# Three edits to the expert stage of a fused attention, feed-forward and expert kernel

## The chip, the cores and the metric

The kernel runs on one core of a Trainium2 chip. The metric is the time of one launch on the device in microseconds. Five engines work side by side, each through its own instructions in order: TensorE (PE, matrix products and transposes), VectorE (DVE), ScalarE (ACT), GpSimd (POOL, here mainly the issuer of indirect DMAs) and SyncE (SP, the issuer of the plain DMAs). 16 DMA engines move data between the chip's memory and the core.

## The reference, cut to what matters

The change touches the third of three parts. Attention with pooled queries gives 1152 tokens of 512 numbers; a gated feed-forward layer follows; its result `x` goes through eight experts, of which each token uses two:

```python
def _moe2_ref(x, w_gate, w_noise, noise, w1, w2):      # x 1152 x 512, 8 experts, hidden 1024
    noisy_logits = x @ w_gate + np.log1p(np.exp(x @ w_noise)) * noise
    top2 = np.argpartition(-noisy_logits, 2, axis=1)[:, :2]
    top2_w = ...                                       # softmax over the two
    for e in range(E):
        for k in range(2):
            mask = top2[:, k] == e
            h = np.maximum(x[mask] @ w1[e], 0.0)
            out[mask] += top2_w[mask, k, None] * (h @ w2[e])
```

## The kernel before

Routing puts the tokens of each expert into blocks of 128, and the expert stage works through a fixed list of units, `SEQ` (L953). A unit is one expert's weights with one set of blocks. Kind P has two blocks, S one, Q one block and a half block (64 tokens), H a half block alone. The list names for each unit its kind and its place among the columns of the index tables, which routing fills at run time; so the work of a unit depends on its kind only. The first two P work on the experts with most tokens; P 0 to 3, Q 0 to 2, S 0 and H 0 to 3 follow in the order of the list. Before the change that order is P, P, P0, H0, Q0, H1, P1, H2, Q1, H3, P2, Q2, P3, S0. Further units, behind a branch (L1296), run only when routing needs them.

**Weights.** An expert has 4 MB, loaded as eight pieces of 512 KB (`e_dma`, L983): pieces 0 to 3 are the first layer (256 hidden columns each), 4 to 7 the second. The buffers of raw weights are two sets of eight; unit u uses set u % 2, so unit u + 2 can be loaded into a piece's buffer once unit u has read it. Full blocks don't use the raw weights: `wsplit` (L1039) splits a piece into a rounded high part (`w_hi`, a cast on ACT, L106) and a low part (`w_lo`, a subtraction on DVE, L1037), into a ring of six pairs of buffers, and each product is three passes, high by high, high by low, low by high (`PASS`). Half blocks use the raw weights in plain float32, with 64 columns of the array for each of two halves.

**Order.** `units` (L1212) writes out the order of all engines' work by hand: whatever is called earlier stands earlier in each engine's queue. Pieces of P, Q and S form one list, `todo`; while piece n is computed, piece n + LEAD (five on) is split, and for P and S (not Q) the load of the same piece of unit u + 2 is issued right after (L1217 to L1220). H units are not in that list.

**A P or S or Q unit** runs eight pieces: first layer in 0 to 3 (`up_pair` for P, `up_one` for Q and S), second in 4 to 7 (`down`). Q and S transpose the hidden values (`h_trans`, two calls of four transposes; ACT casts the high part, DVE subtracts the low). After piece 5, `next_x` transposes the tokens of the next unit, computes its weights and gathers the tokens of unit u + 3. After piece 4, `finish` scales the previous unit's result on DVE into a buffer, one for even units and one for odd, and POOL adds it to the output by an indirect DMA; each such scatter waits for the one before.

**A half** (in H or Q) has the steps `up_half` (L1142; 16 matmuls twice, each followed by a relu on ACT), `hh_trans` twice (L1153; two transposes each, then a copy) and `down_half` (L1166; 32 matmuls). `up_half` reads raw pieces 0 to 3, `down_half` raw pieces 4 to 7; after each, `reload` issues the loads of these four pieces for unit u + 2. An H does `up_half` twice, `reload`, `hh_trans`, `next_x`, `hh_trans`, `finish`, `down_half`, `reload`. A Q does `up_half` after piece 3, `hh_trans` after piece 5, `down_half` after piece 7.

**Banks.** PSUM has eight banks of 512 float32 per partition: two shared for transposes (`bank`, taken in turn), two for the first layer (`pbank("ph")`, in turn), four for the second (`pbank("py")`). The half's relu results lie in `hs0` and `hs1`, one buffer each, which Q's first layer uses too.

Of the kernel before, what the change touches and what calls it, by code (L numbers as in the profile page):

```python
# [21 lines left out]
def fused_kernel(ctx, tc, q, k, v, w_gate, w_val, w_out, rms_g,  # L22
                 r_gate, r_noise, noise, e_w1, e_w2, out, dbg=None):
    nc = tc.nc
    P = 128
    B, H, S, D = q.shape
# [10 lines left out]
    pe, dve, act, pool, sp = nc.tensor, nc.vector, nc.scalar, nc.gpsimd, nc.sync  # L37
# [896 lines left out]
    def r_index(pl):  # L934
# [11 lines left out]
        for z, kind in enumerate((KH, KQ2)):  # L946
# [3 lines left out]

    RAW = []
    REG = {}
    SEQ = [("P", None)] * 2 + [("P", 0), ("H", 0), ("Q", 0), ("H", 1), ("P", 1), ("H", 2), ("Q", 1), ("H", 3), ("P", 2),  # L953
                               ("Q", 2), ("P", 3), ("S", 0)]
    SEQ = [(a, {"P": ((KP, r), (KP2, r)), "Q": ((KQ, r), (KQ2, r)), "S": ((KS, r),), "H": ((KH, r),)}[a]) for a, r in SEQ]
    NU1 = len(SEQ)
    SEQ += [("P", ((KP, r), (KP2, r))) for r in range(NSTAT[KP], NA)]
    SEQ += [("P", ((KQ, r), (KQ2, r))) for r in range(NSTAT[KQ], NE)]
    SEQ += [("S", ((KS, r),)) for r in range(NSTAT[KS], NE)] + [("S", ((KH, r),)) for r in range(NSTAT[KH], NE)]

    def kind(u):
        return SEQ[u][0]

    def nblk(u):
        return len(SEQ[u][1])

    def half(u, k):
        return kind(u) == "H" or kind(u) == "Q" and k == 1
# [48 lines left out]
    def experts():  # L1017
# [21 lines left out]
        def wsplit(u, i):  # L1039
            w_hi(u, i)  # L1040
            w_lo(u, i)
# [21 lines left out]
        def bank():  # L1063
            tb[0] += 1
            if tb[0] % 2:
                return pst.tile([P, 512], F32, name="xt", tag="T")
            return ptab.tile([P, 512], F32, name="xt", tag="tab")

        def pbank(nm):
            if pm:  # L1070
                return pm[0].tile([P, 512], F32, name=nm, tag=nm, bufs=4 if nm == "py" else 2)
            return ps.tile([P, 512], F32, name=nm, tag="gv0" if nm == "py" else "po", bufs=2)
# [32 lines left out]
        def up_pair(u, i, j):  # L1105
            if j == 0:
                PL[u, i] = pbank("ph")
            w = [x.rearrange("p a (b f) -> p (a b) f", f=256) for x in W[u, i]]
            o = PL[u, i][:, 256 * j:256 * j + 256]
            for z, (a, c) in enumerate(PASS):  # L1110
                for d in range(4):
                    pe.matmul(o, w[a][:, d, j * P:j * P + P], XT[u][c][:, d], start=z + d == 0, stop=z == 2 and d == 3)  # L1112

        def up_evac(u, i):
            hi, lo = (x[:, 2 * i:2 * i + 2].rearrange("p a c -> p (a c)") for x in t_hTT(u))
            act.activation(hi, PL[u, i], AF.Relu)
            dve.scalar_tensor_tensor(lo, PL[u, i], 0.0, hi.bitcast(F32), op0=ALU.max, op1=ALU.subtract)
# [14 lines left out]
        def down(u, i, k):  # L1132
            if (u, "y", k) not in PL:
                PL[u, "y", k] = pbank("py")
            w, x = W[u, i], HTT[u]
            f0 = 2 * (i - 4)
            for z, (a, c) in enumerate(PASS):
                for d in range(2):
                    pe.matmul(PL[u, "y", k], x[c][:, f0 + d, k * P:k * P + P], w[a][:, d],  # L1139
                              start=i == 4 and z + d == 0, stop=i == 7 and z == 2 and d == 1)  # L1140

        def up_half(u, a):  # L1142
            k = nblk(u) - 1
            t = pbank("ph")
            for d in range(4):
                for g in range(2):
                    pe.matmul(t[HB * g:HB * g + HB, 0:256], XH[u][:, d],
                              RAW[u % 2][2 * a + g].rearrange("p a (b f) -> p (a b) f", f=256)[:, d],
                              start=d == 0, stop=d == 3)
            HS[u, "h", a] = mo.tile([P, 512], F32, name="hs", tag=f"hs{a}", bufs=1)[:, 0:256]  # L1150
            act.activation(HS[u, "h", a], t[:, 0:256], AF.Relu)

        def hh_trans(u, a, eng):  # L1153
            if a == 0:
                HH[u] = X2[:, 4 + u % 2, 0:8 * HB].rearrange("p (c t) -> p c t", t=HB)
            pt = bank()
            for j in range(2):
                pe.transpose(pt[:, j * P:j * P + P], HS[u, "h", a][:, j * P:j * P + P], ident)
            o = HH[u][:, 4 * a:4 * a + 4].rearrange("p (g j) t -> p j g t", g=2)
            i = pt[:, 0:2 * P].rearrange("p (j g t) -> p j g t", j=2, g=2)  # L1160
            if eng is act:
                act.copy(o, i)
            else:
                eng.tensor_copy(o, i)

        def down_half(u):  # L1166
            k = nblk(u) - 1
            y = PL[u, "y", k] = pbank("py")
            for c in range(8):
                for g in range(2):  # L1170
                    pe.matmul(y[HB * g:HB * g + HB, 0:256], HH[u][:, c], RAW[u % 2][4 + c // 2][:, c % 2, 256 * g:256 * g + 256],
                              start=c == 0, stop=c == 7)

        def piece(u, i):
            if i >= 4:
                for k in range(nblk(u)):
                    if not half(u, k):
                        down(u, i, k)
            elif kind(u) == "P":
                up_pair(u, i, 0)  # L1180
                up_pair(u, i, 1)
                up_evac(u, i)
            else:
                up_one(u, i)
# [27 lines left out]
        def units(u0, u1, skip=0):  # L1212
            todo = [(u, i) for u in range(u0, u1) if kind(u) != "H" for i in range(8)]

            def split(n):
                if n < len(todo):
                    v, j = todo[n]  # L1217
                    wsplit(v, j)
                    if v + 2 < u1 and kind(v) != "Q":
                        wload(v + 2, j)  # L1220

            def reload(u, js):
                if u + 2 < u1:
                    for j in js:
                        wload(u + 2, j)

            def next_x(u):
                if u + 1 < u1:
                    x_trans(u + 1)
                    weight(u + 1)  # L1230
                    if u + 3 < u1:
                        gather_x(u + 3)

            if not skip:
                for u in range(u0, min(u0 + 2, u1)):
                    gather_x(u)
                    for i in range(8):
                        wload(u, i)
                for n in range(LEAD):
                    split(n)  # L1240
                x_trans(u0)
                weight(u0)
                if u0 + 2 < u1:
                    gather_x(u0 + 2)
            n_ = 0
            for u in range(u0, u1):
                last = u == u1 - 1
                if kind(u) == "H":
                    up_half(u, 0)
                    up_half(u, 1)  # L1250
                    reload(u, range(4))
                    hh_trans(u, 0, dve)
                    next_x(u)
                    hh_trans(u, 1, dve)
                    finish(u - 1)
                    down_half(u)
                    reload(u, range(4, 8))
                    continue
                for i in range(8):
                    if n_ < skip:  # L1260
                        n_ += 1
                        continue
                    piece(u, i)
                    if kind(u) != "P":
                        if i == 2:
                            h_trans(u, 0)
                        if i == 4 - last:
                            h_trans(u, 1)
                    if kind(u) == "Q":
                        if i == 3:  # L1270
                            up_half(u, 0)
                            up_half(u, 1)
                            reload(u, range(4))
                        if i == 5:
                            hh_trans(u, 0, act)
                            hh_trans(u, 1, act)
                        if i == 7:
                            down_half(u)
                            reload(u, range(4, 8))
                    if i == 5:  # L1280
                        next_x(u)
                    if u > max(u0, 1) and i == (1 if last else 5 if kind(u) == "S" else 4):
                        finish(u - 1)
                    split(n_ + LEAD)
                    n_ += 1
            finish(u1 - 1)
# [278 lines left out]
```

## Time and profile before

| | us |
|---|---|
| median of three runs (812.81 to 816.31) | 815.96 |
| the profiled execution | 819.15 |
| its span | 817.4 |
| PE busy | 767.9 (94%) |
| DVE busy | 525.4 (64%) |
| ACT busy | 378.0 (46%) |
| POOL busy | 257.0 (31%) |

The profile is of one execution; the span runs from its first to its last instruction, and the profiled execution's own time adds what lies around it. Busy shares are averages over stages with different limits. "PEclk" is the granted clock of TensorE as a share of 2.4 GHz; it is 1 (2.4 GHz) or 0.5 (1.2 GHz) at any moment, so a share between is a mean over a stretch. A line such as L1158 is a line of the kernel before; arrows read "written from read".

### The profile page before, as it was taken

The page shows a single profiled execution, that of the slowest core. Times are in us where ns is not written, and L with a number is a line of the kernel's source. Part 1 is how long each engine was busy: PE and PEld are TensorE (multiplying, and loading weights), DVE is VectorE, ACT ScalarE, POOL GpSimd, SP SyncE. Part 2 cuts the span into 40 slices and gives each one's busy share as a digit, 9 for nine tenths or more (in the row PEclk, how much of TensorE's full clock was granted, in tenths as well). Part 3 has the DMA queues.
Part 4 walks back from the last instruction along what each step waited for, and adds up shares of the span by engine and source line. Part 5 has one row for each costly group of instructions (what it writes and reads, how often), then busy time and mean ns, then how long its engine had stood idle before and what let it go on. Part 6 is the DMA issues. An engine that isn't in the chain of part 4 may idle for free. (4 is left out here: it accounts for less than half of the span.)

```text
span 817.4 us, 13258 instructions
## 1 busy us (share of the span) xinstructions
PE 767.9 (94%) x5008; PEld 630.6 (77%) x5008; DVE 525.4 (64%) x791; ACT 378.0 (46%) x770; POOL 257.0 (31%) x221
## 2 busy tenths in 40 slices
PE   5999999999999899999999999999998899799993
PEld 4877777787776689988888899979976686488792
DVE  6677678688779865765686545697644354345572
ACT  3556566565667535331333243545434244234451
POOL 7457356358514222221223100102232122221121
PEclk9999999999999999999999999999999999889998
DMA  7354232230133213331231016639979969892612
GB/s 213 89 153 138 60 102 73 59 102 15 45 118 103 64 41 103 103 103 52 87 120 55 1 53 208 218 131 342 341 202 292 309 205 313 278 335 59 201 18 39
DMA packets 72728, 113.28 MB, mean 139 GB/s; under 512 B 7281, under 2 KB 37551, under 8 KB 72656
## 3 DMA queue, kind: packets, MB, share of 16 engines
q1 hardware_dynamic: 67504, 101.55, 38.4%
q0 software_dynamic: 5152, 10.80, 6.1%
q8 instruction: 41, 0.67, 0.3%
q14 instruction: 31, 0.25, 0.1%
HBM read 98.16 MB, written 9.85 MB: 132 GB/s over the span
## 5 line engine op out<-in xcount | busy, mean ns | idle before, releaser
L536 PE MATMUL gv<-XN,ws 128*128 128x256 f32 (+2 forms) x912 | 165.1, 331 | 0.9 <-POOL ws L402 0.9
L536 PEld LDWEIGHTS gv<-XN,ws 128*128 128x128 f32 x912 | 143.8, 189 | 15.0 <-issue 1.8
L1037 DVE TENSOR_TENSOR wz<-raw,wz 128x1024 fp32r<-128x1024 f32 x80 | 96.4, 1223 | 66.2 <-ACT wz L106 65.7
L193 DVE TENSOR_REDUCE Ql<-s 128x1 fp32r<-128x1152 f32 x72 | 97.3, 1355 | 57.2 <-PE s L188 35.3
L204 ACT ACTIVATE et<-st 128x288 f32<-128x288 f32 x288 | 103.5, 417 | 41.3 <-PE st L203 38.9
L1139 PE MATMUL py<-wz,hTT 128*128 128x512 f32 x384 | 98.3, 410 | 0.0
L202 PE MATMUL st<-QH,KT 128*128 128x288 f32 x288 | 92.3, 335 | 2.4 <-ACT et L204 1.0
L106 ACT CAST wz<-raw 128x1024 fp32r<-128x1024 f32 x80 | 81.7, 1046 | 26.9 <-DMA raw<-in_moe_w_dram 21.7
L402 POOL TENSOR_TENSOR ws<-wm,ws 128x1024 fp32r<-128x1024 f32 x18 | 43.9, 2438 | 154.4 <-ACT ws L401 139.5
L1139 PEld LDWEIGHTS py<-wz,hTT 128*128 128x128 f32 x384 | 73.4, 196 | 16.4 <-issue 1.2
L557 PE MATMUL po<-ws,hT 128*128 128x512 f32 x324 | 83.2, 395 | 2.2 <-DVE X L562 2.1
L203 PE MATMUL st<-QlT,KT 128*128 128x288 f32 x288 | 81.8, 298 | 0.0
L229 PE MATMUL av<-et,v 128*64 128x288 f32 x576 | 77.4, 412 | 0.5 <-ACT xT L234 0.5
L202 PEld LDWEIGHTS st<-QH,KT 128*128 128x128 f32 x288 | 54.8, 190 | 21.9 <-issue 12.3
L557 PEld LDWEIGHTS po<-ws,hT 128*128 128x128 f32 x324 | 58.9, 188 | 14.2 <-DVE X L562 3.2
L217 DVE TENSOR_TENSOR es<-es,et 128x576 f32<-128x576 f32 x64 | 62.0, 968 | 1.5
L229 PEld LDWEIGHTS av<-et,v 128*64 128x64 f32 x576 | 38.4, 137 | 27.7 <-issue 3.9
L1112 PEld LDWEIGHTS ph<-xgT,wz 128*128 128x128 f32 x480 | 56.0, 188 | 1.3 <-issue 1.2
L1112 PE MATMUL ph<-xgT,wz 128*128 128x256 f32 x480 | 56.6, 279 | 0.0
L203 PEld LDWEIGHTS st<-QlT,KT 128*128 128x128 f32 x288 | 55.2, 192 | 0.1
L1202 POOL DMA_INDIRECT out_dram<-yo,sidx x16 | 26.3, 1645 | 90.1 <-DVE yo L1201 55.1
L546 ACT CAST hT<-sl 128x256 fp32r<-128x256 f32 (+2 forms) x38 | 18.9, 497 | 74.6 <-DVE sl L545 74.6
(280 smaller groups left out, 1143.9 us busy)
## 6 DMA issues: line engine op xcount, KB each, us to landing
raw<-in_moe_w_dram SPq DMA_DIRECT2D x112, 512.0 KB, 7.0
wraw<-in_moe_w_gate_dram SPq DMA_DIRECT2D x6, 1024.0 KB, 5.1
wraw<-in_moe_w_val_dram SPq DMA_DIRECT2D x6, 1024.0 KB, 5.3
wraw<-in_moe_w_out_dram SPq DMA_DIRECT2D x6, 1024.0 KB, 5.0
kraw<-in_k_dram SPq DMA_DIRECT2D x16, 288.0 KB, 3.8
v<-in_v_dram SPq DMA_DIRECT2D x8, 576.0 KB, 3.9
KT<-KT SPq DMA_DIRECT2D x16, 288.0 KB, 3.1
Qraw<-in_q_dram SPq DMA_DIRECT2D x16, 256.0 KB, 4.3
```

Source lines behind the costliest of these rows:

```text
L106: act.copy(o, i)
L193: dve.tensor_reduce(Ql[p % 3][h][:, c, D:D + 1], t[:, :, 0:384], axis=AX.XY, op=ALU.max, negate=True)
L202: pe.matmul(t[:, 0:NG], KT[p, h][:, cs], QhT[p, h][:, n0:n0 + NG], start=True, stop=False)
L203: pe.matmul(t[:, 0:NG], KT2[h][p % NKT[h]][:, cs], QlT[p, h][:, n0:n0 + NG], start=False, stop=True)
L204: act.activation(et[:, h, :], t[:, 0:NG], AF.Exp, scale=SCALE)
L217: eng.tensor_tensor(acc, acc, e, op=ALU.add)
L229: pe.matmul(av[h * D:(h + 1) * D, 0:NG], V[p][:, h, c, :], ET[p, g, c][:, h, :], start=(c == 0), stop=(c == KC - 1))
L536: pe.matmul(t[:, 0:n], w[a][:, d, j * P:(j + 1) * P], XN[hf][b_][:, d, cs], start=(k_ == 0), stop=(k_ == 11))
L557: pe.matmul(pt, HT[f, hf][a][:, j, c0:c0 + P], w[b_][:, j, :], start=(k_ == 0), stop=(k_ == 5))
L1037: eng.tensor_tensor(lo, RAW[u % 2][i], hi.bitcast(F32), op=ALU.subtract)
L1112: pe.matmul(o, w[a][:, d, j * P:j * P + P], XT[u][c][:, d], start=z + d == 0, stop=z == 2 and d == 3)
L1139: pe.matmul(PL[u, "y", k], x[c][:, f0 + d, k * P:k * P + P], w[a][:, d], start=i == 4 and z + d == 0, stop=i == 7 and z == 2 and d == 1)
```

## The change

`SEQ` is put in another order: P, P, P0, P1, H0, P2, H1, P3, Q0, H2, Q1, H3, Q2, S0. In a Q, `up_half` (both) and the reload of pieces 0 to 3 come before piece 0, one `hh_trans` before piece 1 and one before piece 2, `down_half` and the reload of pieces 4 to 7 before piece 3. In an H, `hh_trans` writes into the two first-layer banks instead of the two shared for transposes.

```diff
@@ -950,8 +950,8 @@
 
     RAW = []
     REG = {}
-    SEQ = [("P", None)] * 2 + [("P", 0), ("H", 0), ("Q", 0), ("H", 1), ("P", 1), ("H", 2), ("Q", 1), ("H", 3), ("P", 2),
-                               ("Q", 2), ("P", 3), ("S", 0)]
+    SEQ = [("P", None)] * 2 + [("P", 0), ("P", 1), ("H", 0), ("P", 2), ("H", 1), ("P", 3), ("Q", 0), ("H", 2), ("Q", 1),
+                               ("H", 3), ("Q", 2), ("S", 0)]
     SEQ = [(a, {"P": ((KP, r), (KP2, r)), "Q": ((KQ, r), (KQ2, r)), "S": ((KS, r),), "H": ((KH, r),)}[a]) for a, r in SEQ]
     NU1 = len(SEQ)
     SEQ += [("P", ((KP, r), (KP2, r))) for r in range(NSTAT[KP], NA)]
@@ -1153,7 +1153,7 @@
         def hh_trans(u, a, eng):
             if a == 0:
                 HH[u] = X2[:, 4 + u % 2, 0:8 * HB].rearrange("p (c t) -> p c t", t=HB)
-            pt = bank()
+            pt = pbank("ph") if kind(u) == "H" else bank()
             for j in range(2):
                 pe.transpose(pt[:, j * P:j * P + P], HS[u, "h", a][:, j * P:j * P + P], ident)
             o = HH[u][:, 4 * a:4 * a + 4].rearrange("p (g j) t -> p j g t", g=2)
@@ -1260,23 +1260,22 @@
                     if n_ < skip:
                         n_ += 1
                         continue
+                    if kind(u) == "Q":
+                        if i == 0:
+                            up_half(u, 0)
+                            up_half(u, 1)
+                            reload(u, range(4))
+                        if i in (1, 2):
+                            hh_trans(u, i - 1, act)
+                        if i == 3:
+                            down_half(u)
+                            reload(u, range(4, 8))
                     piece(u, i)
                     if kind(u) != "P":
                         if i == 2:
                             h_trans(u, 0)
                         if i == 4 - last:
                             h_trans(u, 1)
-                    if kind(u) == "Q":
-                        if i == 3:
-                            up_half(u, 0)
-                            up_half(u, 1)
-                            reload(u, range(4))
-                        if i == 5:
-                            hh_trans(u, 0, act)
-                            hh_trans(u, 1, act)
-                        if i == 7:
-                            down_half(u)
-                            reload(u, range(4, 8))
                     if i == 5:
                         next_x(u)
                     if u > max(u0, 1) and i == (1 if last else 5 if kind(u) == "S" else 4):
```

## Rows read from the trace of the kernel before

**Rows 1.** By stretch: window, length, busy PE PEld DVE ACT POOL, PEclk, DMA share, GB/s

```profile
...
599.40:609.25 9.85, 8.91 (x77) 5.59 (x76) 4.41 (x9) 2.62 (x5) 3.57 (x3) 1.00 0.93 254
609.25:633.50 24.25, 22.14 (x154) 17.26 (x154) 9.19 (x12) 9.95 (x15) 6.67 (x5) 0.93 1.00 302
633.50:647.63 14.13, 10.77 (x78) 6.32 (x74) 4.75 (x10) 2.77 (x5) 2.89 (x3) 0.88 0.92 305
...
670.24:680.10 9.86, 8.92 (x78) 5.59 (x77) 4.42 (x9) 2.63 (x5) 2.67 (x2) 1.00 0.69 227
680.10:704.20 24.10, 22.38 (x154) 17.40 (x154) 9.25 (x12) 9.85 (x15) 7.67 (x6) 0.93 0.99 297
704.20:721.94 17.74, 12.59 (x78) 7.54 (x74) 4.75 (x10) 2.77 (x5) 3.52 (x3) 0.71 0.85 290
...
744.90:769.57 24.67, 22.92 (x157) 17.65 (x155) 13.58 (x17) 12.14 (x18) 4.07 (x2) 0.93 0.38 111
...
791.97:805.10 13.13, 12.38 (x81) 10.87 (x79) 6.30 (x8) 4.94 (x7) 3.29 (x3) 1.00 0.35 47
sum 228.60, PE 211.89 PEld 169.84 DVE 112.06 ACT 90.42 POOL 52.51; mean PE 17.66 PEld 14.15 DVE 9.34 ACT 7.54 POOL 4.38
```

**Rows 2.** Waits of PE, 576 to 806: total us, times, longest

```profile
PE xt L1158 <- ACT hs L1151: 7.3, 2, 4.6
PE xt L1158 <- DVE hTT L1007: 5.5, 3, 2.1
PE xt L1158 <- DVE xgT L1007: 2.5, 4, 0.9
PE xt L1002 <- ACT hs L1130: 0.7, 1, 0.7
...
```

**Rows 3.** PE in order of time, Q0: start, us, instruction, [idle before]

```profile
609.25 4.36 PE L1127 MATMUL ph<-wz,xgT 128*128 128x256 f32 x36
613.45 0.60 PE L1002 MATMUL xt<-ident,hs 128*128 128x128 f32 x4
613.80 1.66 PE L1127 MATMUL ph<-wz,xgT 128*128 128x256 f32 x12
615.39 3.67 PE L1147 MATMUL ph<-raw,X 128*64 128x256 f32 x32
618.99 1.66 PE L1139 MATMUL py<-wz,hTT 128*128 128x512 f32 x6
...
624.80 0.44 PE L1158 MATMUL xt<-ident,hs 128*128 128x128 f32 x2 [2.11 <-DVE hTT L1007]
...
630.01 3.67 PE L1171 MATMUL py<-raw,X 128*64 128x256 f32 x32
```

**Rows 4.** ACT in order of time, in H1 and H3

```profile
638.37 1.04 ACT L106 CAST wz<-raw 128x1024 fp32r<-128x1024 f32 x1 [8.78 <-DMA raw<-in_moe_w_dram]
639.32 0.65 ACT L1151 ACTIVATE hs<-ph 128x256 f32<-128x256 f32 x2
...
711.10 1.04 ACT L106 CAST wz<-raw 128x1024 fp32r<-128x1024 f32 x1 [11.59 <-DMA raw<-in_moe_w_dram]
```

**Rows 5.** SP in order of time, in Q0: issues of loads

```profile
617.36 2.73 SPq L990 DMA_DIRECT2D raw<-in_moe_w_dram  x4
```

**Rows 6.** DMA queues, 590 to 650: packets, MB, share of 16 engines

```profile
q1 hardware_dynamic: 10732, 13.14, 67.3%
q0 software_dynamic: 1100, 2.45, 18.6%
```

**Rows 7.** Loads issued 617 to 620: count, size, median us to landing

```profile
raw<-in_moe_w_dram SPq DMA_DIRECT2D x4, 512.0 KB, 5.6
```

**Rows 8.** Loads issued 640 to 649

```profile
raw<-in_moe_w_dram SPq DMA_DIRECT2D x9, 512.0 KB, 10.1
```

**Rows 9.** All scatters of line 1202

```profile
DMA to landing us min/median/max: 3.8/5.7/8.7
```

**Rows 10.** Chain of waits at the end: start, us, what

```profile
800.45 5.26 DMA out_dram<-yo,sidx
```

## The prediction

> **What bounds the kernel now.** I read the page first: PE is busy 94% of the span, so only what PE loses can be won. Its slices are full until the last third, the expert stage, so I cut that stage at the first matmul of each unit, from PE's order of time, and asked for the sums of each stretch [rows 1]. From 576.5 us on the units run P0, H0, Q0, H1, P1, H2, Q1, H3, P2, Q2, P3, S0; the rows are H0, Q0, H1, H2, Q1, H3, Q2, S0 and the sum of all twelve, 228.60 us. The four P, which is the sum less these eight, take 228.60 - 51.58 (four H) - 73.02 (three Q) - 13.13 = 90.87 us. An H takes 9.85 us where its clock stays at 1.00, but 14.13 and 17.74 us where it follows a Q, at 0.88 and 0.71. Every Q runs at 0.93.
>
> Then PE's waits over these stretches [rows 2]. They name what is late: 7.3 us in two waits for a half's relu on ACT (hs), 5.5 us in three for the last cast of a hidden transpose (hTT), 2.5 us in four for the last cast of the next unit's tokens (xgT), all three ahead of the halves' transposes of line 1158; and 0.7 us in the last unit. That is 16.0 us of idle; the rest of the loss is clock.
>
> Why the relu is late stands in ACT's order of time [rows 4]: at 638.37 and 711.10 a weight cast (L106) starts after 8.78 and 11.59 us of waiting for its load, and the two relus of the H come right behind it, 0.65 us for both. ACT works in order, so a late load holds relus that need no load. The load is late because unit u+2 is loaded into the buffers of unit u, and a Q gives them up only when its half has read them, the last four after piece 7. PE's order for Q0 shows it [rows 3]: the half's first layer begins at 615.39, its second at 630.01, 3.5 us from the unit's end, where the cast of the next unit's piece 4 is due as well.
>
> **The change, part by part.**
>
> *Half first.* In a Q the half's first layer (32 matmuls, 3.67 us) moves ahead of piece 0, its transposes ahead of pieces 1 and 2, its second layer (3.67 us) ahead of piece 3. Nothing is added: the same matmuls, copies and 8 loads. The clock of a Q from its start, with 4.36 us for three first-layer pieces, 1.66 for one, 1.66 for a second-layer piece (pipelined about 1.45 and 1.5) and 0.35 for a transpose group [rows 3]: half's first layer 0 to 3.6; piece 0 to 5.1; half's transposes and pieces 1 and 2 to 8.6; hidden transpose to 9.0; half's second layer to 12.6; piece 3 to 14.0; four second-layer pieces with transposes between them to 20.4. In Q0 before, the first load followed the start of the half's first layer by 1.97 us (617.36 against 615.39) [rows 3, 5]. So the first four are now issued from 2.0 us of the unit instead of 8.1, the last four from 9.9 instead of 21.6. Four loads issued together landed in a median of 5.6 us [rows 7]. The first cast of the next weights stands behind piece 3, at 14.0, and its load landed at about 7; the cast that blocked, behind piece 7, stands at 20.4 and its load, issued at 9.9, lands at about 16. Both waits go. The 5.5 us for the bank of the hidden transpose go too, since the half's transposes now come before it.
>
> What is late next: piece 6, at 17.6, wants the second hidden transpose, whose two casts stand behind a weight cast on ACT (1.04 us [rows 4]) and its subtraction on DVE. I get 17.8 for the low part, which is used a third of the way into the piece: cost 0, with 0.3 us of cover; without that cover up to 0.7 us a Q.
>
> *Halves' transposes of an H in the first layer's banks.* This takes away the 2.5 us on xgT. Those banks are emptied by the relus that the transposes need anyway, so no wait is added. In an H before a P two token blocks pass through DVE ahead of the copy of the second transpose, about 0.6 us later than the second layer's later half wants it: 2 x 0.6 = 1.2 us come back. Bounds 0 and 2 x 0.94 (what H0 loses now, 9.85 less 8.91 busy [rows 1]).
>
> *Order.* P0, P1, H0, P2, H1, P3, Q0, H2, Q1, H3, Q2, S0. No work is added, and the transposes of the next unit's tokens are as many as before. What moves is the demand on the DMA: Q0, H2, Q1 and H3 issue 8 loads each, 32 in some 60 us. The price of one: the loads' queue took 67.3% and the software queue 18.6% of the engines while the first moved 13.14 MB in 60 us [rows 6]. So 0.524 MB takes 0.673 x 60 / 13.14 x 0.524 = 1.61 us alone, and 1.61 x 85.9 / 67.3 = 2.06 us beside gathers and scatters; 302 GB/s in Q0 [rows 1] makes it 1.74. The tightest place is Q1. With Q0's start as zero, H2 starts at 20.8 (a mean clean Q, below) and issues from 22.8; eight loads for H3, then four for Q2, the last of them due 19.1 us into Q1, at 48.9. A first landing after 4 us leaves 22.1 us for eleven more: 2.0 us each is just in time. In a crowded stretch nine loads landed after a median of 10.1 us [rows 8]; with 1 us between issues the fifth then lands 14 us after the first issue, 2.5 us a load. Bounds: nothing (a clean stretch holds no wait that could go as well), and 11 x 0.5 = 5.5 us of idle, 9 with the clock: H3 lost 17.74 - 9.1 = 8.6 us on 5.15 of idle [rows 1], 1.7 per us. I take 3, near what 2.06 gives with some unevenness.
>
> The Trainium skill (DMA: Bandwidth & Descriptors, Queues, rings and completion order) speaks against packing loads here: each DMA engine takes turns, a packet at a time, between all queues that have work. The trace does not show equal turns, 67.3 to 18.6 [rows 6], and by it the 3 us stand; what equal turns would make is the third rival.
>
> *Scatters.* Each waits for the one before; they landed after 3.8 to 8.7 us, median 5.7 [rows 9]. Four of them, those of P3 and Q0, must be through before DVE writes Q1's result into the same buffer. At 9 us each they end some 52 us after Q0's start, and that write comes at about 56: cost 0, up to 2 if each takes 1.5 us more. The end is kept: the scatter before the last landed at 800.45 + 5.26 = 805.71 [rows 10], 0.6 us after S0's end, and from there to the span's end stays as it is.
>
> **The sum.** A clean stretch is PE's busy time less what the clock took (1 - PEclk, times its length) [rows 1]. Q0 22.14 - 1.70 = 20.4, Q1 20.7, Q2 21.2: 62.3 against 73.02, 10.7 gained. H0 and H2 8.9 each, H1 10.77 - 1.70 = 9.1, H3 taken like H1 (it idled at the low clock too): 36.0 against 51.58, 15.6 gained. P and S0 stay. 26.3 - 1.2 - 3 = 22 us. The profiled execution took 819.15 us, so 797 by it; the median of the runs before, 815.96, is 3.2 below, and for the median I forecast 794.
>
> **Rivals.** *One: the H after a Q still wait.* The loads come earlier, but in a burst and among gathers, so casts still wait for them at a Q's end and hold the next relus. For: ACT waited 8.78 and 11.59 us, not 1 [rows 4]. Against: the blocking loads move by 12 us. H2 and H3 then lose what H1 and H3 lose now, 13.7 us; the rest, 26.3 - 13.7 - 1.2, is about 11: 805.
>
> *Two: the change does not do what it says.* The half's copies now stand among Q's first casts, the hidden transposes fall behind, and piece 6 waits where the half's transpose waited: each Q keeps its 3.6 us, and H2 and H3 lose as above. For: PE stood still for 2.11 us at one such place [rows 3] and the Q fell to 0.93. Against: ACT is busy 9.95 of 24.25 us in Q0 [rows 1]. Gain 26.3 - 10.7 - 13.7, 0 to 3: 814.
>
> *Three, on the other side: slower.* Place: the 32 loads from Q0 on. If gathers and scatters, nearly always under way there, took every second turn of the engines, a load takes 2 x 1.74 = 3.5 us; the last lands 6 + 31 x 3.5 = 114 us after Q0's start, S0 ends 10 us later, at 124, against 93 planned. Of 25 us won 31 are lost: 822. It decides at 3.3 us a load (6 + 31 x 3.3 + 10 = 93 + 25). Such turns are the rule cited above. Against: 2.06 with both queues at work.
>
> **How the numbers follow.** Forecast 0.70, rival one 0.15, two 0.08, three 0.07. The forecast's own range is 789 (the reserve unspent, and a median 2 us lower: the three runs lie 3.5 apart) to 801 (10 us of waits instead of 3). For 8 in 10 the range goes on through rival one with its scatter: 789 to 809. A difference over 0.5%, 4.1 us, can be told from none. Faster by that: the forecast, rival one and a sliver of two, 0.86; within it 0.07; slower 0.07.
>
> **What would show it.** Right: H2 and H3 near 9 us at a clock of 1.00, each Q near 21, the twelve stretches near 206; no cast on ACT waiting over 2 us for a load; PE's waits on hs and hTT gone; a Q's first load some 2 us after its first matmul. Wrong: relus of H2 or H3 behind a cast that a load released (rival one); a wait of piece 6 on hTT in each Q (two); loads landing more than 3 us apart from Q0 on (three). H0 or H1 over 10.5 us would put the part on the banks wrong.

## The result and the profile after

The changed kernel takes 794.62 us (median of four runs, 793.75 to 794.80) against 816.13 for the kernel before (four runs, 812.81 to 819.16): ratio 0.9735, 95% interval 0.9697 to 0.9774. The forecast was 794, in a range of 789 to 809. The profiled execution took 794.49 us, with a span of 792.6 against 817.4.

The same cut by unit, from the first matmul of P0, P1, H0, P2, H1, P3, Q0, H2, Q1, H3, Q2, S0; columns as in [rows 1]:

```profile
576.54:599.64 23.10, 23.10 (x154) 21.14 (x152) 15.24 (x20) 10.99 (x14) 3.69 (x2) 1.00 0.93 297
599.64:622.81 23.17, 23.17 (x150) 20.59 (x148) 14.10 (x18) 10.40 (x13) 5.66 (x6) 1.00 0.80 236
622.81:631.95 9.14, 8.89 (x77) 5.62 (x76) 3.79 (x9) 1.84 (x4) 2.25 (x3) 1.00 1.02 294
631.95:655.18 23.23, 23.23 (x150) 20.69 (x148) 13.11 (x16) 10.39 (x13) 8.76 (x6) 1.00 1.00 319
655.18:664.32 9.14, 8.89 (x77) 5.63 (x76) 3.78 (x9) 1.84 (x4) 1.54 (x3) 1.00 0.96 325
664.32:688.00 23.68, 23.68 (x154) 21.19 (x152) 13.79 (x17) 10.88 (x14) 7.89 (x5) 1.00 0.77 238
688.00:708.68 20.68, 20.68 (x153) 16.05 (x152) 9.05 (x13) 11.29 (x17) 1.86 (x2) 1.00 0.65 217
708.68:717.35 8.67, 8.67 (x77) 5.72 (x78) 6.25 (x11) 2.02 (x5) 4.08 (x4) 1.00 0.89 235
717.35:738.00 20.65, 20.65 (x155) 16.01 (x151) 9.06 (x12) 11.08 (x17) 3.65 (x3) 1.00 1.07 350
738.00:746.67 8.67, 8.67 (x78) 5.72 (x79) 5.31 (x11) 2.33 (x5) 3.23 (x2) 1.00 0.88 283
746.67:767.08 20.41, 20.41 (x155) 16.34 (x151) 8.83 (x13) 11.03 (x17) 5.21 (x3) 1.00 0.51 163
767.08:780.20 13.12, 12.40 (x81) 10.86 (x79) 8.95 (x10) 5.97 (x8) 3.28 (x3) 1.00 0.21 27
sum 203.66, PE 202.43 PEld 165.56 DVE 111.27 ACT 90.08 POOL 51.12; mean PE 16.87 PEld 13.80 DVE 9.27 ACT 7.51 POOL 4.26
```

Length and PE's busy time are now the same number nearly everywhere, and the clock is 1.00 in every stretch. The sum fell from 228.60 [rows 1] to 203.66, by 24.94; the span by 24.8. So all of the change lies in these stretches. By kind: four H 51.58 to 35.62, three Q 73.02 to 61.74, S0 13.13 to 13.12, and four P 90.87 to 93.18, which is the one term that grew.

What PE, and then ACT, still waits for between 565 and 790 (total us, times, longest), against the 16.0 us of [rows 2]:

```profile
PE xt L1002 <- ACT hs L1130: 0.7, 1, 0.7
PE py L1171 <- DVE X L1164: 0.5, 2, 0.3
...
ACT wz L106 <- DMA raw<-in_moe_w_dram: 0.2, 1, 0.2
```

The waits on hs, hTT and xgT ahead of line 1158 are gone, and casts wait 0.2 us in all for loads, not 8.78 and 11.59 [rows 4]. PE in Q0, in order of time, and SP's first issue in it:

```profile
688.00 3.67 PE L1147 MATMUL ph<-raw,X 128*64 128x256 f32 x32
691.61 1.68 PE L1127 MATMUL ph<-wz,xgT 128*128 128x256 f32 x12
...
696.92 3.67 PE L1171 MATMUL py<-raw,X 128*64 128x256 f32 x32
700.52 1.68 PE L1127 MATMUL ph<-wz,xgT 128*128 128x256 f32 x12
...
705.75 3.00 PE L1139 MATMUL py<-wz,hTT 128*128 128x512 f32 x12
708.68 3.67 PE L1147 MATMUL ph<-raw,X 128*64 128x256 f32 x32
```

```profile
689.97 2.73 SPq L990 DMA_DIRECT2D raw<-in_moe_w_dram  x4
```

The first load leaves 1.97 us after the unit's first matmul, as worked out, and the half's second layer begins at 8.9 us of the unit (forecast 9.0). The next H starts with no gap behind the last piece.

### The profile page after: what moved, and what is told of

Its sections match the earlier page's. It is cut to its first block, busy times and chain, and to the rows that moved or that the text cites. A ratio compares the mean times of both kernels' runs of the same rounds, so it can differ in the third digit from the quotient of the medians.

```text
span 792.6 us, 13276 instructions
## 1 busy us (share of the span) xinstructions
PE 758.6 (96%) x5008; PEld 626.4 (79%) x5008; DVE 525.9 (66%) x791; ACT 377.8 (48%) x770; POOL 255.2 (32%) x221
## 5 line engine op out<-in xcount | busy, mean ns | idle before, releaser
L1139 PE MATMUL py<-wz,hTT 128*128 128x512 f32 x384 | 93.5, 395 | 0.0
L1139 PEld LDWEIGHTS py<-wz,hTT 128*128 128x128 f32 x384 | 70.2, 188 | 13.9
L1112 PEld LDWEIGHTS ph<-xgT,wz 128*128 128x128 f32 x480 | 57.9, 188 | 1.0 <-issue 0.8
L1112 PE MATMUL ph<-xgT,wz 128*128 128x256 f32 x480 | 58.4, 282 | 0.0
```

## The experiments

The kernel before was run beside each group; ratios are to it. The theory: a Q that reads its half's weights late releases their buffers late, the load of the next unit in that set comes late, and ACT's in-order queue passes the wait on to relus and transposes.

**The parts by themselves.** Six of the combinations of half first, order and banks; the seventh is the change.

Each takes its hunks from the change as they stand; the three hunks begin

```diff
-    SEQ = [("P", None)] * 2 + [("P", 0), ("H", 0), ("Q", 0), ("H", 1), ("P", 1), ...
+    SEQ = [("P", None)] * 2 + [("P", 0), ("P", 1), ("H", 0), ("P", 2), ("H", 1), ...
...
-            pt = bank()
+            pt = pbank("ph") if kind(u) == "H" else bank()
...
+                    if kind(u) == "Q":
+                        if i == 0:
+                            up_half(u, 0)
```

and stand for order, banks and half first.

> Half first alone: the old order of units and the old banks. Theory (the gain is the earlier release of a Q's weight buffers): Q falls to about 21 us, the two H after a Q lose their wait for a load, and only the waits on the shared transpose banks stay (0.9 us in each of four H). Gain 20 to 22 us, 795 to 797, ratio to before near 0.975. Rival A (the order of units does it, by spreading the loads): most of H1's and H3's 5.0 and 8.6 us stay and the gain is 8 to 12, 804 to 808. Rival B (half first helps only with the new banks): under 8.

> Half first and the new banks, with the old order of units. Theory: as fast as the full change or faster, since the order adds nothing to the loads' release and puts three P on odd places, whose first layers ran 0.4 to 0.6 us longer each in the trace after (11.68 to 11.79 us against 11.17): 792 to 795, ratio 0.971 to 0.974. Rival A (the order is needed): 798 or more, with ACT waiting for loads in H1 and H3.

> Half first and the new order, with the old banks for an H's transposes. Theory: each of four H waits on the shared banks again, 0.9 us before a Q and 0.7 to 1.2 before a P, no clock lost: 797.5 to 799. Rival B (the banks carry the change): 805 or more.

> The new order alone, with half late and the old banks. Theory: a Q still releases its buffers late, so H2 and H3 keep a wait for a load (5 to 9 us each) and every Q its 3.5 us; H0 and H1 follow a P and lose 0.9 to 1.2; P1 to P3 run 0.4 to 0.6 us slower: no gain, 814 to 820, ratio 0.998 to 1.005. Rival A (the order spreads the loads): 806 or less.

> The new banks alone. Theory: the waits on xgT go, 0.9 us in H0 and H2 and 0.7 in H1 and H3; the relus behind a load's cast stay late: gain 2 to 4 us, 811 to 814, ratio 0.995 to 0.998. Rival B (the banks carry the change): under 806.

> The new order and the new banks with half late. Theory: as the order alone, less 3 us for the banks: 811 to 817. Rival A or B: under 806.

| kernel | median us (range) | ratio, 95% interval |
|---|---|---|
| half first | 796.95 (795.46 to 797.18) | 0.9756, 0.9734 to 0.9778 |
| half first and banks | 792.61 (792.30 to 793.64) | 0.9714, 0.9693 to 0.9735 |
| half first and order | 798.49 (797.18 to 798.83) | 0.9781, 0.9760 to 0.9802 |
| order alone | 811.43 (809.88 to 812.26) | 0.9929, 0.9906 to 0.9953 |
| banks alone | 809.97 (807.90 to 814.00) | 0.9929, 0.9899 to 0.9959 |
| order and banks | 809.04 (807.30 to 810.57) | 0.9906, 0.9869 to 0.9944 |
| the change | 794.62 (793.75 to 794.80) | 0.9735, 0.9697 to 0.9774 |

Half first carries the change: 2.4% of 2.65% alone. In its trace (576 to 790 us) PE waits for nothing but what the banks were to remove, and for the relu in S0:

```profile
PE xt L1158 <- DVE xgT L1007: 3.1, 4, 0.9
PE xt L1002 <- ACT hs L1130: 0.7, 1, 0.7
```

The shares depend on the order in which the parts are added: put last, on top of order and banks, half first takes the ratio from 0.9906 to 0.9735, 1.7%. The banks add 0.4% to half first. The order takes 0.2 to 0.3% away again where the half is first, with the old banks and with the new: half first and banks without the order is the fastest of the seven (beside it ran, in the same group, a kernel that turned out to be the change again, below: 793.73 to 795.22, no overlap). The first three expectations held. The last three did not: order alone and banks alone each gained 0.7%, where nothing and 0.2 to 0.5% were expected, and both together 0.9%.

Why the order alone helps is seen in its trace. First the stretches Q0 and H2, then ACT around the start of H2:

```profile
689.54:714.78 25.24, 22.28 (x153) 17.28 (x153) 11.26 (x14) 10.58 (x16) 3.96 (x4) 0.93 0.44 118
714.78:724.59 9.81, 8.87 (x79) 5.54 (x75) 5.37 (x10) 3.57 (x6) 3.18 (x3) 1.00 1.05 323
```

```profile
716.51 1.05 ACT L106 CAST wz<-raw 128x1024 fp32r<-128x1024 f32 x1 [7.40 <-DMA raw<-in_moe_w_dram]
717.46 0.38 ACT L1151 ACTIVATE hs<-ph 128x256 f32<-128x256 f32 x1
```

The cast still waits 7.40 us, but ends 2.8 us after H2's first matmul; in H1 before it ended at 639.41, 5.9 us after the first matmul at 633.50 [rows 1, 4]. The half's first layer of 3.6 us covers the one and not the other. The load came sooner: the cast starts 4.1 us after SP issued the first of the four loads (712.40), against 7.5 before (630.88). The DMA engines were 0.44 busy in this Q, not 1.00 as in Q0 before [rows 1], and from 712.0 to 713.5 they moved 4 packets, against 341 from 630.5 to 631.5 before. By the kernel's text the reason is that the Q is now followed by an H and a Q, and splitting a Q's pieces issues no loads (L1219), while before the same pieces belonged to a P, and its splits issued loads among the late ones. So the order spreads the loads, as rival A had it, but only where the half is late did that gain anything. Its price shows in PE's waits:

```profile
PE xt L1158 <- DVE hTT L1007: 9.1, 3, 4.4
```

That is 9.1 us against 5.5 [rows 2] for the hidden transposes inside the Q's, where casts now wait instead. With the banks alone the waits on xgT went, as expected, and PE's two waits for a relu fell from 7.3 [rows 2] to 3.5 us, while those on hidden transposes rose from 5.5 to 6.3; why the loads came earlier against PE's order there I did not isolate.

**Late issue, first try.** To put the loads back at their old place I moved the two `reload` calls alone, from ahead of pieces 0 and 3 to behind pieces 3 and 7.

```diff
-                            reload(u, range(4))
...
-                            reload(u, range(4, 8))
...
+                    if kind(u) == "Q":
+                        if i == 3:
+                            reload(u, range(4))
+                        if i == 7:
+                            reload(u, range(4, 8))
```

> The full change, but a Q issues the loads of the next unit in its set where it did before: four after piece 3, four after piece 7, though its half has long read them. Same work in the same order on every compute engine. Theory: ACT's weight cast at the end of Q waits for its load again and holds the relus of H2 and H3: 4 to 9 us come back in each of H2 and H3 with the clock, and some in Q: 803 to 812. Rival C (the gain is the new place of the half's transposes, ahead of the hidden ones): under 2 us come back, 794 to 797.

793.97 us (793.73 to 795.22), ratio 0.9733 (0.9712 to 0.9755). That looks like a win for rival C and is none: the trace shows the first load of Q0 at 689.27, 1.98 us after its first matmul at 687.29, and the fifth at 697.34, 10.05 us after it; in the change these were 1.97 and 10.04. SP has its own queue. Here a load left when its buffer's last reader was done, wherever its call stood, since nothing else stood between in SP's queue. The edit did not move the loads, and the run is a repeat of the change.

**Late issue, second try.** This time PE reads the buffers late: eight transposes of raw weights in Q0 and in Q1 that do no work.

```diff
+        def hold(u, js, t):
+            for j in js:
+                pe.transpose(t[:, 2 * P:3 * P], RAW[u % 2][j][:, 0, 0:P], ident)
...
+                    if kind(u) == "Q" and u + 2 < u1:
+                        if i == 3:
+                            hold(u, range(4), PL[u, "y", 1])
+                            reload(u, range(4))
+                        if i == 7:
+                            hold(u, range(4, 8), PL[u, "y", 1])
+                            reload(u, range(4, 8))
```

> The full change, with eight extra transposes of raw weights in Q0 and in Q1 (four after piece 3, four after piece 7) that do no work but read the buffers, so that the loads cannot start before the place they had before the change. The extra transposes cost 8 x 0.09 x 2 = 1.4 us. Theory (loads): casts on ACT wait for loads after piece 3 and at the end of Q0 and Q1, the relus of H2 and H3 come late, the clock falls: some 4 us in each Q and 5 in each H, 18 + 1.4, 806 to 815. Rival C (only the place of the half's transposes counts): 795 to 797.

> The full change with the same eight extra transposes in Q0 and Q1, but four right before the half's first transposes and four right after its second layer, so that the buffers are held 1.5 us longer at most. Both theories: only their own time, 1.4 us, 795.5 to 797; anything above 799 would mean that the extra transposes cost more than their time and that the run with the buffers held late proves nothing.

Held late: 809.19 us (805.02 to 811.94), ratio 0.9919 (0.9890 to 0.9948). Held right after the half (four calls in `hh_trans`, four behind `down_half`): 795.92 us (795.14 to 796.38), ratio 0.9773 (0.9748 to 0.9798). With the buffers held a little the extra transposes cost 1.3 us over the change's 794.62 (run in another group), about the 1.4 expected; held late the same transposes bring back 13 us on top. Every compute engine has the same work in both. In the total the expectation held, by unit only in part: in the profiled execution Q0 and Q1 are 3.2 and 5.2 us longer than in the change (0.7 of each for the transposes), near the 4 expected, but H2 and H3 only 2.2 and 1.6, not 5; the mean clock fell in Q1 alone, to 0.93. The trace of the first, ACT and then PE's waits:

```profile
706.45 1.04 ACT L106 CAST wz<-raw 128x1024 fp32r<-128x1024 f32 x1 [3.08 <-DMA raw<-in_moe_w_dram]
...
716.80 1.04 ACT L106 CAST wz<-raw 128x1024 fp32r<-128x1024 f32 x1 [3.83 <-DMA raw<-in_moe_w_dram]
717.75 0.65 ACT L1151 ACTIVATE hs<-ph 128x256 f32<-128x256 f32 x2
```

```profile
PE ph L1158 <- ACT hs L1151: 3.7, 2, 2.2
PE py L1139 <- ACT hTT L1005: 3.1, 2, 1.8
PE py L1139 <- DVE hTT L1007: 1.3, 2, 0.6
```

The pair of rows at 716.80 and 717.75 is the pattern of [rows 4]: a cast released by a load, and both relus at once behind it, 0.65 us. The theory holds: a late release of the buffers alone brings most of the loss back, and the wait passes through ACT's queue to PE. Held late, the change is no faster than order and banks with the half at its old place (0.9919, of which the extra transposes are 0.002, against 0.9906): in this order of units the new place showed no gain that can be told without the early release.

**The loads taken away.** The kernel before, with the loads that its Q issue left out:

```diff
                         if i == 3:
                             up_half(u, 0)
                             up_half(u, 1)
-                            reload(u, range(4))
...
                             down_half(u)
-                            reload(u, range(4, 8))
```

> The kernel before, with the 24 loads that its three Q issue left out, so that the next unit in that set computes with old weights; all else as before. Theory (two causes): H1 and H3 fall from 14.1 and 17.7 to some 10 us, since no cast waits for a load, while each Q keeps most of its 3.5 us, which came from the order of transposes and casts: 803 to 807. Rival A (order of units or banks alone): above 811. If loads were all, 796.

803.26 us (801.18 to 804.31), ratio 0.9861 (0.9826 to 0.9896), inside 803 to 807. PE's waits, and the stretches of Q0 and H1:

```profile
PE xt L1158 <- DVE hTT L1007: 5.1, 3, 1.7
PE xt L1158 <- DVE xgT L1007: 3.1, 4, 0.9
...
```

```profile
609.09:631.62 22.53, 20.82 (x154) 16.27 (x154) 10.28 (x13) 10.60 (x16) 6.79 (x5) 1.00 0.77 221
631.62:641.42 9.80, 9.05 (x78) 5.61 (x74) 3.61 (x9) 1.94 (x4) 1.93 (x2) 1.00 1.05 349
```

H1 falls from 14.13 to 9.80 without any load to wait for, and no wait for a half's relu is left; but 1.7 us in each Q stays. One part of the expectation missed: Q0 fell from 24.25 to 22.53, so it kept about half of its loss and not most of it: its stall stayed (1.7 us, after 2.1), but at a clock of 1.00 instead of 0.93. So in the order of before there were two causes: late loads, and the half's transposes that stood behind the hidden ones for a bank. By this run loads are some 12 us of the 21. That is an estimate, since the run takes away the 24 loads themselves, 12.6 MB, and not only their lateness; the rest, by subtraction, is the place of the half inside the Q and the banks.

**What the order costs.** P's first layers of 96 matmuls, first in the kernel before, then after:

```profile
576.51 11.47 PE L1112 MATMUL ph<-xgT,wz 128*128 128x256 f32 x96
647.63 11.16 PE L1112 MATMUL ph<-xgT,wz 128*128 128x256 f32 x96
721.94 11.17 PE L1112 MATMUL ph<-xgT,wz 128*128 128x256 f32 x96
769.57 11.17 PE L1112 MATMUL ph<-xgT,wz 128*128 128x256 f32 x96
```

```profile
576.54 11.47 PE L1112 MATMUL ph<-xgT,wz 128*128 128x256 f32 x96
599.64 11.68 PE L1112 MATMUL ph<-xgT,wz 128*128 128x256 f32 x96
631.95 11.79 PE L1112 MATMUL ph<-xgT,wz 128*128 128x256 f32 x96
664.32 11.78 PE L1112 MATMUL ph<-xgT,wz 128*128 128x256 f32 x96
```

Nothing waits in them. What differs is the unit's number: before, all four P had even numbers (2, 6, 10, 12), after, P1 to P3 have 3, 5, 7, and odd units keep their transposed tokens in another pair of buffers. The test gives all units the even pair:

```diff
-                XT[u] = [(mo if u % 2 else wps[0]).tile(..., tag=f"xgT{z}" if u % 2 else ("wm", "ws20")[z]) ...]
+                XT[u] = [wps[0].tile(..., tag=("wm", "ws20")[z]) for z in range(2)]
```

> The full change, with the transposed tokens of every unit in the one pair of buffers that even units use (odd units have another pair). Theory D (the first layers of P1 to P3 run at 120 to 121 ns a matmul in the full change because those units now stand on odd places, against 113 to 118 on even ones, and that is what the order costs): P1, P2, P3 fall to 11.2 to 11.5 us, gain 0.8 to 2.1 us, 792.5 to 794. Rival (the loads that are under way slow the matmuls): first layers stay at 11.7 to 11.8, 794.6.

793.17 us (791.60 to 793.41), ratio 0.9737 (0.9711 to 0.9762). The ratio can't tell it from the change, since the kernel before scatters too much; the lengths can:

```profile
576.52 11.47 PE L1111 MATMUL ph<-xgT,wz 128*128 128x256 f32 x96
599.62 11.47 PE L1111 MATMUL ph<-xgT,wz 128*128 128x256 f32 x96
631.67 11.16 PE L1111 MATMUL ph<-xgT,wz 128*128 128x256 f32 x96
663.43 11.16 PE L1111 MATMUL ph<-xgT,wz 128*128 128x256 f32 x96
```

(The line is one less because the edit is one line shorter.) P1 to P3 gain 1.46 us together, and the span 1.6, 791.0 against 792.6. So the place of the operand makes the matmuls slower, not the order as such. The other traces agree: in all 14 kernels the first layers of P from unit 1 on took 11.68 to 11.79 us from the odd pair and 11.10 to 11.57 from the even pair, and unit 1 itself, an odd P before the stage's twelve stretches, went from 11.69 in the change to 11.47 with one place. Why P0 takes 11.47 in all kernels, and P1 here, stays open, and so does what it is about the place.

**A faster version.** Half first and banks in the old order, and one more edit:

```diff
-                        if i == 4 - last:
+                        if i == 4:
                             h_trans(u, 1)
```

> Half first and the new banks in the old order of units, and in the last unit the second hidden transpose after piece 4 instead of piece 3, so that its 0.7 us wait for a relu is covered by that piece. Expected 0.3 to 0.7 us under the same kernel without that last edit, which ran at 792.6: 791.9 to 792.6 and about 2 us under the full change. If piece 6 then waits for the low part of the transpose instead, 792.6 or more.

792.85 us (792.02 to 794.12), ratio 0.9709 (0.9675 to 0.9743). The 0.7 us wait of S0 is gone from PE's waits, which are down to 0.5 us in all; the time is not below that of half first and banks (792.61), so the expected 0.3 to 0.7 us did not come in any way that can be told. In the profiled executions S0 takes 12.2 us from its first to its last matmul, against 13.1, but P2's first layer, which the edit does not touch, took 11.57 us against 11.15, and the stage began 0.3 us later. Both are some 2 us under the change. With PE at a clock of 1.00 and 0.5 us of waits, a new order has next to no waits left to remove in this stage.

## Why the prediction was right

**The mechanism** held step by step: the loads leave at 1.97 us of the Q, casts no longer wait for them, the waits on hs, hTT and xgT ahead of the halves' transposes are gone, and the clock is 1.00 in every stretch of the stage. The held buffers bring the pattern back; that cause is shown, not only argued. How much of the gain is the release and how much the half's new place is an estimate, and the two do not simply add.

**The terms of the sum**, as far as stretches show them: Q gained 11.3 us (10.7 in the sum). H gained 16.0 against 15.6 less 1.2; of the two waits of 0.6 us that were to come back in an H before a P, two of 0.25 us came. The 3 us held back for late loads were not spent: ACT waited 0.2 us. The step that failed is "P and S0 stay": P took 2.31 us more, 1.75 of it in the first layers (44.97 to 46.72 us), for a reason that no row of before suggested, since there every P from P0 on had an even number; the other 0.56 is not explained. A P on an odd number did stand before that stretch, outside the rows that I read: unit 1, whose first layer took 11.68 us at 553.15.

**The time** came out within 1 us of the forecast by luck, because two errors met. By the profiled execution the gain is 819.15 - 794.49 = 24.7 us, not 22; by the medians it is 21.5. The profiled execution of before stood at the upper end of its runs (812.81 to 819.16), that of after in the middle of its own. I had carried the difference to the median, 3.2 us, over to the forecast as if the new kernel kept it. By the stretches the sum was 2.9 us too small: it had 0.6 too little for Q, 1.6 for H and 3 for the unspent reserve, and 2.3 too much for P. The 2.9 and the 3.2 nearly cancel. The range did not need that luck.

**The rivals.** One, that H still waits, fell: H2 and H3 take 8.67 us. Two, that the wait moves to piece 6, fell: no wait on hTT is left, though the held run shows that it is where a late load goes first (3.1 and 1.3 us). Three was a pace of 3.3 us a load from Q0 on. The queues from 708 to 748 us, columns as in [rows 6]:

```profile
q1 hardware_dynamic: 8229, 10.22, 74.8%
q0 software_dynamic: 1017, 1.96, 21.8%
```

0.748 x 40 / 10.22 x 0.524 = 1.53 us a load alone and 1.98 beside gathers and scatters, what Q1 needed (2.0) and near the 2.06 taken from before. The rule of the Trainium skill (DMA: Bandwidth & Descriptors, Queues, rings and completion order) did not make itself felt here as equal time: 74.8 to 21.8. What the Trainium skill states there is turns by packet and not time, and no row here shows whether the second queue always had work waiting.

## What to carry to other kernels

When a buffer's last reader decides when the next load may leave, move that reader first; here the place of the call that issues the load did not matter. The late load cost PE time because its cast stood in an in-order queue ahead of short work that PE needs, so read what came right behind the cast that waited. And before parts of a change are kept together, time each alone and with the others: here one part helped only as long as another was missing, and cost 1.5 to 2 us once it was there.

## What the runs showed of the hardware that was not expected

The same wait was followed by a low clock in one kernel's execution and not in another's. In the kernel before, Q1 stood still for 1.7 us (of the 5.5 in three waits of [rows 2] the longest, 2.1, was Q0's) and had a mean clock of 0.93 over its stretch [rows 1]; without the Q's loads, Q0 and Q1 stood still for as long (the 1.7 of the waits above) at 1.00. The twelve matmuls that follow the wait in Q1, before and then without the Q's loads:

```profile
696.18 4.61 PE L1139 MATMUL py<-wz,hTT 128*128 128x512 f32 x12
689.97 3.02 PE L1139 MATMUL py<-wz,hTT 128*128 128x512 f32 x12
```

So the clock's share of a stall is no fixed price.

Some kernels in which casts wait for loads scatter more from run to run: 6.9 us with the buffers held late and 6.1 for the banks alone (ten runs each), against 1.0 to 1.8 (four to six runs) for the change, half first, half first and banks, half first and order, buffers held a little and one place. That makes no rule: the order alone, where casts waited 19.0 us in all for loads, scattered by 2.4 in ten runs, and the kernel without the Q's loads, where no cast waits for one, by 3.1 in four. What makes the difference was not tried.

The same 96 matmuls take 11.16 to 11.79 us without any wait, and which buffers their moving operand lies in accounts for part of it.
